# Keeping the high part of u divided by 4096, and writing the low part of the first product's weights at once

## The chip, the cores and the metric

The kernel runs on one core of a Trainium2 chip. The core has TensorE (PE; its weight loads are listed apart as PEld and run beside the products), VectorE (DVE), ScalarE (ACT), GpSimd (POOL) and SyncE (SP), whose queue issues the DMAs. Each engine works through its own queue in order, and engines wait for one another by semaphores. The metric is the device time of one execution in microseconds (us). Five runs of the kernel before gave a median of 676.99 us, from 675.87 to 677.44.

## The reference: what is computed

Two blocks follow each other, all in fp32. The first is attention with a decay, in blocks of 64 positions:

```python
Dmask = np.where(rel >= 0, lam[:, None, None] ** rel[None, :, :], 0.0)
for b in range(nb):
    intra = np.einsum('bhic,bhjc->bhij', qb, kb) * Dmask[None]
    intra = np.einsum('bhij,bhjd->bhid', intra, vb)
    inter = np.einsum('bhid,bhde->bhie', qb * lam_pow[None], kv_state)
    out[:, :, sl] = intra + inter
    kv_state = lam_block * kv_state + np.einsum('bhsd,bhse->bhde', kb_dec, vb)
```

Its result x (4 batches, 768 positions, 512 channels) goes through a low-rank mixer over the positions and a two-layer net over the channels:

```python
h = x.transpose(0, 2, 1) @ U @ V
u = x + h.transpose(0, 2, 1)
ch = np.maximum(u @ w_ch1, 0.0) @ w_ch2
return u + ch
```

The inputs `U`, `V`, `w_ch1` and `w_ch2` are float64 and reach the kernel as pairs of 32-bit words.

## The kernel before, in words

**The split products.** The two large products run in the type fp32r[...]. So each operand is split: for u the high part `t` is u with its low 12 bits cleared (mask `HI`), and the low part is u - t; the weights likewise. With E = 2^-12 the first product u @ w_ch1 is put together from two sums, each in its own PSUM bank:

- `pz` adds w_high * u_high and (4096 w_low) * u_low;
- `pd` adds D_w * D_u, where D_w = w_low - E w_high and D_u = E u_high - u_low.

The result is (1 + E) pz + 4096 pd: multiplied out, the terms that are not wanted cancel, and the four partial products of u and w are left.

**Stages.** There are 24 tiles of 128 positions, s = 0 to 23, six to a batch (NT). Each tile goes through attention (`prep`, `scale`, `scores`, `inter`, `masked`, `intra`, `state`), then through the mixer (`low` once per batch, `low_rows`, `mix`), then through `turn`, which transposes u and splits it. Then the first product runs over 16 blocks of its 2,048 columns (ft) and 6 groups of 512 positions (g), two groups at a time: `hidden(ft, pair)` is one unit of 24 matmuls. Its results (`rs`) go to DRAM and come back for the second product.

**Order.** Up to the end of the first units (`ordered.close()`, L787) the order on each engine is that of the code, written out by hand in `pieces` (L541 to L561): in step s, `prep(s + 1)`, `mix(s - 7)`, `intra(s)`, `state(s)`, `turned`, `scores(s + 1)` and so on. From s = 8 each step also turns one tile. At s = 6, 12 and 18, the first tiles of a batch, the low-rank work of the batch before comes in between: `low` on TensorE, `low_rows` on VectorE (L469), and then `spread` (ScalarE, L480 and L481), `low_part` (VectorE, L475) and `spread_low` (ScalarE, L484). After `ordered.close()` a planner orders the instructions.

**`turn(s)`, L502.** Four transposes write u to PSUM (`pt`), and VectorE masks it into `t`. What follows has two forms. In the first four groups (s = 0 to 15, `g < FG`) VectorE writes the low part from PSUM (L527), and the function `rest` is put off to the next step's `turned`: ScalarE makes `te` = E t (L531) and copies t into the high part `hi` (L532), and GpSimd writes D_u, `diff` = te - low (L533). In the last two groups (s = 16 to 23) VectorE writes D_u (L520), ScalarE copies `hi` (L522) and u itself (L523), and GpSimd makes the low part (L524). `hi` and `low` are slices of the group's tile `u_hl`, 4 runs of 128 elements each, and `diff` of the tile `u_d`; `te` is a tile of its own in the pool slot `tmp`, which has three buffers that `t`, `te`, `uf` and the mixer's `p_h` share.

**The weights.** `weight_steps` (L104) turns the pairs of words into fp32: two masks on VectorE (L153, L154), two ScalarE steps for the exponent (L159, L160), three more on VectorE (L170, L178, L183). `split_steps` (L189) adds the split for w_ch1 and w_ch2 alike: `five` masks the high part (L201) and has ScalarE copy it into the weight tile (L204), `six` subtracts in place (L208) and has ScalarE write 4096 times the result (L209), `seven` makes D_w (L212). The w_ch1 tiles have three buffers (`w1_pool`), the w_ch2 tiles go to DRAM and come back. In attention `aside` issues these steps, and `on_scalar` puts their ScalarE part off to `late` of a following step.

**`hidden`, L695.** After the 16 `pz` matmuls of a unit (L709) ScalarE scales `pz` into `rs` (L715); after the 8 `pd` matmuls (L719) VectorE adds 4096 `pd` (L724), and SP stores the result (L725). The PSUM banks alternate from unit to unit.

Of the kernel before, what the change touches and what calls it, by code (L numbers as in the profile page):

```python
# [8 lines left out]
FP32 = mybir.dt.float32  # L9
# [3 lines left out]
ALU = mybir.AluOpType  # L13

P = 128
# [3 lines left out]
def kernel(  # L19
# [9 lines left out]
    moe_w_ch2: bass.AP,  # L29
    out: bass.AP,  # L30
):

# [12 lines left out]
    nc = tc.nc  # L47
# [16 lines left out]
    E = 2.0**-12  # L64
# [15 lines left out]
    def on_scalar(what):  # L80
        if late and late[0] is None:
            late.append(what)
        else:
            what()
# [12 lines left out]
    def tmp(name):  # L97
        return wconv.tile([P, C], FP32, tag="tmp", bufs=3, name=name)
# [87 lines left out]

        return fetches + [one, two, three, four]

    def split_steps(tile_of, src, in_parts=False):  # L189

        st = {}

        def dst():
            if "w" not in st:
                st["w"] = wconv.tile([P, C], FP32, tag="wf", name="wf")
            return st["w"]

        def five():
            st["t"] = t = wconv.tile([P, C], FP32, tag="wt", name="wt")
            st["o"] = o = tile_of()  # L200
            nc.vector.tensor_scalar(  # L201
                t.bitcast(U32), st["w"].bitcast(U32), HI, None, ALU.bitwise_and
            )
            on_scalar(lambda: nc.scalar.copy(o[:, 0, :], t))  # L204

        def six():
            w = st["w"]
            nc.vector.tensor_tensor(out=w, in0=w, in1=st["t"], op=ALU.subtract)  # L208
            on_scalar(lambda: nc.scalar.mul(st["o"][:, 1, :], w, 4096.0))  # L209

        def seven():
            nc.vector.scalar_tensor_tensor(  # L212
                st["o"][:, 2, :], st["t"], -E, st["w"], ALU.mult, ALU.add
            )

        return weight_steps(dst, src, C, in_parts=in_parts) + [five, six, seven]
# [3 lines left out]
    def w1_steps(ft, in_parts=False):  # L220
        def tile_of():
            w1v[ft] = w1_pool.tile([P, 3, C], F32R, tag="w1", name="w1")
            return w1v[ft]

        cols = moe_w_ch1[:, ft * P : (ft + 1) * P].rearrange("(c p) f -> p c f", p=P)
        return split_steps(tile_of, cols, in_parts)
# [3 lines left out]
    keep = mix_ctx.enter_context(tc.tile_pool(name="keep", bufs=1, side="right"))  # L230
# [12 lines left out]
    def one_bank(shape, name, tag):  # L243
        return psf.tile(shape, FP32, tag=tag, name=name)
# [4 lines left out]
    def bank(shape, name, tag):  # L249
        return psa[0].tile(shape, FP32, tag=tag, bufs=2, name=name)  # L250
# [72 lines left out]
    st = {}  # L323
# [178 lines left out]
    def turn(s):  # L502

        g, n = divmod(s, TG)
        if n == 0:
            uhl[g] = hl_at[g >= FG].tile([P, 2, CT, N], F32R, tag="hl", name="u_hl")
            ud[g] = d_at[g >= FG].tile([P, CT, N], F32R, tag="d", name="u_d")
        cols = slice(n * P, (n + 1) * P)
        pt = one_bank([P, CT, P], "put", "pt") if g < FG else bank([P, CT, P], "put", "b1")
        for ct in range(CT):  # L510
            nc.tensor.transpose(  # L511
                out=pt[:, ct, :], in_=xs[s][:, ct * P : (ct + 1) * P], identity=ident
            )
        nc.sync.dma_start(out=u_d[s], in_=xs.pop(s))
        t = tmp("ut").rearrange("p (c n) -> p c n", n=P)
        nc.vector.tensor_scalar(t.bitcast(U32), pt.bitcast(U32), HI, None, ALU.bitwise_and)
        hi, low, diff = uhl[g][:, 0, :, cols], uhl[g][:, 1, :, cols], ud[g][:, :, cols]
        if g >= FG:

            nc.vector.scalar_tensor_tensor(diff, t, 1.0 + E, pt, ALU.mult, ALU.subtract)  # L520
            uf = tmp("uf").rearrange("p (c n) -> p c n", n=P)
            nc.scalar.copy(hi, t)  # L522
            nc.scalar.copy(uf, pt)  # L523
            nc.gpsimd.tensor_tensor(out=low, in0=uf, in1=t, op=ALU.subtract)  # L524
            return

        nc.vector.tensor_tensor(out=low, in0=pt, in1=t, op=ALU.subtract)  # L527

        def rest():
            te = tmp("te").rearrange("p (c n) -> p c n", n=P)  # L530
            nc.scalar.mul(te, t, E)  # L531
            nc.scalar.copy(hi, t)  # L532
            nc.gpsimd.tensor_tensor(out=diff, in0=te, in1=low.bitcast(FP32), op=ALU.subtract)  # L533

        turned[s] = rest

# [5 lines left out]
    for s in range(NS):  # L542
        b, c = divmod(s, NT)
# [20 lines left out]
    def load_next(name, engine=nc.sync):  # L564
# [5 lines left out]
        "prep": prep, "fade": fade, "scores": scores, "masked": masked, "inter": inter,  # L570
        "intra": intra, "state": state,
        "low": low, "low_rows": low_rows, "next_of_low": next_of_low, "mix": mix, "turn": turn,
        "scale": scale, "turned": lambda s: turned.pop(s)(),
    }
# [112 lines left out]
    def banks(n, other):  # L687

        tags = ("b1", "b2") if other else ("a1", "a2")
        pzs, pds = ([bank([P, N], name, tag) for i in range(n)] for name, tag in zip(("pz", "pd"), tags))  # L690
        return list(zip(pzs, pds))
# [3 lines left out]
    def hidden(ft, pair, before={}):  # L695

        acc = dict(zip(pair, banks(len(pair), next(turns))))
        count = iter(range(12 * len(pair)))

        def others():  # L700
            for what, s in before.get(next(count), ()):
                run[what](s)

        w = w1v[ft].rearrange("p n (c f) -> p n c f", f=P)
        for ct in range(CT):
            for n in range(2):
                for g in pair:
                    others()
                    nc.tensor.matmul(  # L709
                        out=acc[g][0], lhsT=w[:, n, ct, :], rhs=uhl[g][:, n, ct, :],  # L710
                        start=(ct == 0 and n == 0), stop=(ct == CT - 1 and n == 1),
                    )
        rs = {g: r_pool.tile([P, N], FP32, tag="r", name="r") for g in pair}
        for g in pair:
            nc.scalar.mul(rs[g], acc[g][0], 1.0 + E)  # L715
        for ct in range(CT):
            for g in pair:
                others()
                nc.tensor.matmul(  # L719
                    out=acc[g][1], lhsT=w[:, 2, ct, :], rhs=ud[g][:, ct, :],  # L720
                    start=(ct == 0), stop=(ct == CT - 1),
                )
        for g in pair:
            nc.vector.scalar_tensor_tensor(rs[g], acc[g][1], 4096.0, rs[g], ALU.mult, ALU.add)  # L724
            nc.sync.dma_start(out=r_d[ft][g], in_=rs[g])  # L725

    def w2_steps(ft):
        def tile_of():
            w2v[ft] = w2_pool.tile([P, 3, C], F32R, tag="w2", name="w2")
            return w2v[ft]  # L730

        def keep():
            nc.sync.dma_start(out=w2_d[ft], in_=w2v.pop(ft).bitcast(FP32))

        return split_steps(tile_of, moe_w_ch2[ft * P : (ft + 1) * P, :]) + [keep]


    w2hl, w2dd = {}, {}
# [15 lines left out]
    def run_units(units, side, every=lambda i: None):  # L754
        for i, (pair, ft) in enumerate(units):
            hidden(ft, pair)
            for step in side[len(side) * i // len(units) : len(side) * (i + 1) // len(units)]:
                step()
            every(i)
# [18 lines left out]
    for i, (pair, ft) in enumerate(head):  # L778
        before = {}
        for unit, n, *piece in rest:  # L780
            if unit == i:
                before.setdefault(n, []).append(piece)
        hidden(ft, pair, before)
        for n, step in side:
            if n == i:
                step()
# [9 lines left out]
    for ft in range(3, FT - 1):  # L796
        side += w1_steps(ft) + w2_steps(ft - 3)
    side += w2_steps(FT - 4)
    run_units(body, side)
    side = w1_steps(FT - 1)  # L800
    for ft in range(LAST, FT):
        side += w2_steps(ft)
# [8 lines left out]
    rs, ms = {}, {}  # L811
# [17 lines left out]
    acc = {}  # L829
# [50 lines left out]
    for i, (pair, ft) in enumerate(tail[6:]):  # L880
        hidden(ft, pair)
        if i < 2:
            for n in range(2):
                w2_back(backs.pop(0))
        if i == 0:
            for n in range(3):
                fetch(n)
        if i == 1:
            for n in range(2):
                split(n)  # L890

    STAG = 3
    for i in range(len(steps) - STAG):
        g, ft = steps[i]
# [49 lines left out]
```

## Time and profile before

| What | us |
|---|---|
| Median of five runs | 676.99 |
| The profiled execution, its whole time | 676.99 |
| Its span, first to last instruction | 674.9 |
| Attention and mixer, up to the first `pz` matmul | 0 to 123.4 |
| First product, its units alone | 152 to 400.2 |
| Second product | 400.5 to the end |

How to read the profile: times are from the start of the span. A row of a group gives line, engine, operation, output and input by the program's names, shape and count, then the busy time and the mean of one in ns, then the idle time just before them and what ended it. The chain of waits is followed back from the last instruction: at each step to what released it, or to its predecessor on the same engine. A row of the timeline gives start, length, engine, line and what is computed; consecutive instructions of one kind are drawn together (x32), and a bracket names idle time before the row and what ended it. The ends of matmuls are modelled, so starts are the surer numbers.

Two more groups of the page, the longest on VectorE and ScalarE, belong to the second product and to the first one's `rs`:

```profile
L825 DVE SCALAR_TENSOR_TENSOR m<-rm,m 128x512 fp32r<-128x512 f32 x96 | 71.5, 746 | 47.5 <-ACT m L824 47.1
...
L715 ACT ACTIVATE r<-pz 128x512 f32<-128x512 f32 x96 | 52.0, 593 | 58.8 <-PE pz L709 58.2
```

The granted TensorE clock was full throughout (mean 1.000).

### The profile page before, as it was taken

The page shows a single profiled execution, that of the slowest core. Times are in us where ns is not written, and L with a number is a line of the kernel's source. Part 1 is how long each engine was busy: PE and PEld are TensorE (multiplying, and loading weights), DVE is VectorE, ACT ScalarE, POOL GpSimd, SP SyncE. Part 2 cuts the span into 40 slices and gives each one's busy share as a digit, 9 for nine tenths or more (in the row PEclk, how much of TensorE's full clock was granted, in tenths as well). Part 3 has the DMA queues.
Part 4 walks back from the last instruction along what each step waited for, and adds up shares of the span by engine and source line. Part 5 has one row for each costly group of instructions (what it writes and reads, how often), then busy time and mean ns, then how long its engine had stood idle before and what let it go on. Part 6 is the DMA issues. An engine that isn't in the chain of part 4 may idle for free.

```text
span 674.9 us, 13222 instructions
## 1 busy us (share of the span) xinstructions
PE 666.5 (99%) x5124; PEld 545.3 (81%) x5124; DVE 499.5 (74%) x879; ACT 293.1 (43%) x545; POOL 113.8 (17%) x92
## 2 busy tenths in 40 slices
PE   9999999999999999999999999999999999999997
PEld 8988898787888888888888888888888888888885
DVE  4689999777999777777797255786686776865864
ACT  4666878555665544444455121232232322322320
POOL 4556667330000000000000000030030300300300
PEclk9999999999999999999999999999999999999999
DMA  9999884164777655555577999854363363543521
GB/s 206 218 234 240 216 220 126 62 224 155 239 261 242 223 202 203 202 203 203 202 266 255 327 322 388 287 171 148 96 210 102 110 203 94 163 149 95 169 81 63
DMA packets 131776, 131.28 MB, mean 195 GB/s; under 512 B 81346, under 2 KB 89794, under 8 KB 131714
## 3 DMA queue, kind: packets, MB, share of 16 engines
q1 hardware_dynamic: 130656, 130.18, 61.1%
q8 instruction: 40, 0.66, 0.4%
q10 hardware_dynamic: 1058, 0.26, 0.2%
q14 instruction: 22, 0.18, 0.1%
HBM read 80.09 MB, written 50.33 MB: 193 GB/s over the span
## 4 chain that ended last, share of the span: by engine, by line
PE 94%; DVE 3%; ACT 2%; issue 0%; DVEq 0%; ACTq 0%
PE pz L709 27%; PE pz L843 13%; PE pz L841 13%; PE pd L719 13%; PE pd L845 13%; PE pss L388 3%; PE px L441 3%; PE put L511 2%; PE pq L343 1%; PE pkv L406 1%; PE px L429 1%; PE pk L343 1%; PE pp L456 1%; PE pu L494 1%; DVE sm L397 1%
## 5 line engine op out<-in xcount | busy, mean ns | idle before, releaser
L709 PE MATMUL pz<-u_hl,w 128*128 128x512 f32 x768 | 190.5, 397 | 0.0
L709 PEld LDWEIGHTS pz<-u_hl,w 128*128 128x128 f32 x768 | 144.0, 188 | 35.5 <-issue 0.4
L841 PE MATMUL pz<-w_hl,m 128*128 128x512 f32 x384 | 151.6, 396 | 0.0
L843 PE MATMUL pz<-w_hl,m 128*128 128x512 f32 x384 | 151.6, 396 | 0.0
L845 PE MATMUL pd<-w_d,m 128*128 128x512 f32 x384 | 150.0, 396 | 0.0
L824 ACT ACTIVATE m<-mt 128x512 fp32r<-128x512 f32 x96 | 60.7, 632 | 196.8 <-PE pd L845 138.5
L825 DVE SCALAR_TENSOR_TENSOR m<-rm,m 128x512 fp32r<-128x512 f32 x96 | 71.5, 746 | 47.5 <-ACT m L824 47.1
L870 POOL TENSOR_TENSOR o<-o,u 128x512 f32<-128x512 f32 x20 | 29.8, 1524 | 447.4 <-DVE o L866 447.4
L724 DVE SCALAR_TENSOR_TENSOR r<-pd,r 128x512 f32<-128x512 f32 x96 | 61.8, 686 | 53.2 <-ACT r L715 43.6
L719 PE MATMUL pd<-u_d,w 128*128 128x512 f32 x384 | 98.6, 397 | 0.0
L843 PEld LDWEIGHTS pz<-w_hl,m 128*128 128x128 f32 x384 | 72.3, 188 | 17.7
L845 PEld LDWEIGHTS pd<-w_d,m 128*128 128x128 f32 x384 | 72.3, 188 | 17.6
L841 PEld LDWEIGHTS pz<-w_hl,m 128*128 128x128 f32 x384 | 72.3, 188 | 17.6
L719 PEld LDWEIGHTS pd<-u_d,w 128*128 128x128 f32 x384 | 72.1, 188 | 17.3
L715 ACT ACTIVATE r<-pz 128x512 f32<-128x512 f32 x96 | 52.0, 593 | 58.8 <-PE pz L709 58.2
L823 DVE TENSOR_SCALAR mt<-rm 128x512 uint32<-128x512 uint32 x96 | 46.2, 481 | 33.0 <-DMA rm<-r_d 32.7
L826 DVE SCALAR_TENSOR_TENSOR m<-m 128x512 fp32r<-128x512 f32 x96 | 69.1, 720 | 0.9
L204 ACT CAST w<-wt 128x512 fp32r<-128x512 f32 x32 | 19.9, 622 | 40.9 <-DVE wt L201 33.7
L397 DVE TENSOR_TENSOR sm<-pss,mask 128x512 f32<-128x512 f32 x48 | 30.8, 683 | 5.8 <-PE pss L388 5.7
L371 POOL TENSOR_TENSOR qs<-qt,powq 128x512 f32<-128x512 f32 x20 | 26.0, 1298 | 24.3 <-ACT qt L346 21.9
L159 ACT ACTIVATE sc<-sc,ends 128x512 f32<-128x512 uint32 x30 | 21.7, 723 | 18.3 <-DVE sc L153 18.3
L441 PEld LDWEIGHTS px<-vraw,sm 128*64 128x64 f32 x768 | 24.6, 137 | 5.9 <-issue 2.6
(84 smaller groups left out, 710.8 us busy)
## 6 DMA issues: line engine op xcount, KB each, us to landing
r_d<-r SPq DMA_DIRECT2D x96, 256.0 KB, 2.5
rm<-r_d SPq DMA_DIRECT2D x96, 256.0 KB, 2.7
words<-in_moe_w_ch_dram SPq DMA_DIRECT2D x30, 512.0 KB, 4.4
w_d<-w SPq DMA_DIRECT2D x16, 768.0 KB, 3.3
w_hl<-w_d SPq DMA_DIRECT2D x16, 512.0 KB, 6.2
vraw<-in_v_dram SPq DMA_DIRECT2D x24, 256.0 KB, 4.3
u_d<-x_nat SPq DMA_DIRECT2D x24, 256.0 KB, 3.4
u<-u_d SPq DMA_DIRECT2D x24, 256.0 KB, 3.9
```

Of the source, the lines that this page charges most:

```text
L441: nc.tensor.matmul(out=px[half[t], x, a, :], lhsT=sm[:, x, a, half[t]], rhs=vr[:, 2 * a + x, :], start=(first and a == 0), stop=(a == HP - 1),
L709: nc.tensor.matmul(out=acc[g][0], lhsT=w[:, n, ct, :], rhs=uhl[g][:, n, ct, :], start=(ct == 0 and n == 0), stop=(ct == CT - 1 and n == 1),)
L715: nc.scalar.mul(rs[g], acc[g][0], 1.0 + E)
L719: nc.tensor.matmul(out=acc[g][1], lhsT=w[:, 2, ct, :], rhs=ud[g][:, ct, :], start=(ct == 0), stop=(ct == CT - 1),)
L724: nc.vector.scalar_tensor_tensor(rs[g], acc[g][1], 4096.0, rs[g], ALU.mult, ALU.add)
L823: nc.vector.tensor_scalar(t.bitcast(U32), r.bitcast(U32), HI, None, ALU.bitwise_and)
L824: nc.scalar.activation(out=m[:, 0], in_=t, func=AF.Relu)
L825: nc.vector.scalar_tensor_tensor(m[:, 1], r, 0.0, hi, ALU.max, ALU.subtract)
L826: nc.vector.scalar_tensor_tensor(m[:, 2], hi, E, low, ALU.mult, ALU.subtract)
L841: nc.tensor.matmul(out=pz, lhsT=m[:, 0, cols], rhs=hl[:, 0], start=first, stop=False)
L843: nc.tensor.matmul(out=pz, lhsT=m[:, 1, cols], rhs=hl[:, 1], start=False, stop=end)
L845: nc.tensor.matmul(out=pd, lhsT=m[:, 2, cols], rhs=dd, start=first, stop=end)
```

## The change

The high part of u is kept as E u_high, made by one ScalarE multiplication in place of the copy, in both forms of `turn`. GpSimd then takes the high part itself to make D_u, and `te` is gone. In turn the low part of w_ch1 is kept as it is, not times 4096, so both terms of `pz` are smaller by 4096, and `rs` is scaled by 4096 + 1 instead of 1 + E. Since it needs no factor any more, VectorE's subtraction in `six` writes the low part of w_ch1 straight into the weight tile, and `seven` reads it from there. For w_ch2 nothing changes: `w2_steps` passes scale=4096.0 and keeps the ScalarE step.

```diff
-    def split_steps(tile_of, src, in_parts=False):
+    def split_steps(tile_of, src, in_parts=False, scale=None):
...
         def six():
-            w = st["w"]
-            nc.vector.tensor_tensor(out=w, in0=w, in1=st["t"], op=ALU.subtract)
-            on_scalar(lambda: nc.scalar.mul(st["o"][:, 1, :], w, 4096.0))
+            w, low = st["w"], st["o"][:, 1, :]
+            st["low"] = low.bitcast(FP32) if scale is None else w
+            nc.vector.tensor_tensor(
+                out=low if scale is None else w, in0=w, in1=st["t"], op=ALU.subtract
+            )
+            if scale is not None:
+                on_scalar(lambda: nc.scalar.mul(low, w, scale))

         def seven():
             nc.vector.scalar_tensor_tensor(
-                st["o"][:, 2, :], st["t"], -E, st["w"], ALU.mult, ALU.add
+                st["o"][:, 2, :], st["t"], -E, st["low"], ALU.mult, ALU.add
             )
...
-            nc.scalar.copy(hi, t)
+            nc.scalar.mul(hi, t, E)
             nc.scalar.copy(uf, pt)
...
         def rest():
-            te = tmp("te").rearrange("p (c n) -> p c n", n=P)
-            nc.scalar.mul(te, t, E)
-            nc.scalar.copy(hi, t)
-            nc.gpsimd.tensor_tensor(out=diff, in0=te, in1=low.bitcast(FP32), op=ALU.subtract)
+            nc.scalar.mul(hi, t, E)
+            nc.gpsimd.tensor_tensor(
+                out=diff, in0=hi.bitcast(FP32), in1=low.bitcast(FP32), op=ALU.subtract
+            )
...
-            nc.scalar.mul(rs[g], acc[g][0], 1.0 + E)
+            nc.scalar.mul(rs[g], acc[g][0], 4096.0 + 1.0)
...
-        return split_steps(tile_of, moe_w_ch2[ft * P : (ft + 1) * P, :]) + [keep]
+        rows = moe_w_ch2[ft * P : (ft + 1) * P, :]
+        return split_steps(tile_of, rows, scale=4096.0) + [keep]
```

## The prediction

> **What bounds the kernel now.** I read the busy shares first, then the shares of the chain that ended last.
>
> ```profile
> PE 666.5 (99%) x5124; PEld 545.3 (81%) x5124; DVE 499.5 (74%) x879; ACT 293.1 (43%) x545; POOL 113.8 (17%) x92
> ...
> PE 94%; DVE 3%; ACT 2%; issue 0%; DVEq 0%; ACTq 0%
> ```
>
> TensorE is the bound: it is busy nearly throughout, and the chain runs over it for 94% of the span. So time can only come from the other 6%. The chain in order of time shows where that lies: from 105.08 to the last VectorE additions at 669.93 every piece is a TensorE piece (a pair of two products, 24 matmuls, takes 3.75 + 1.88 = 5.62 us, over and over). ScalarE stands in the chain between 41 and 105 us only. The place to see is the start of the third batch of attention (s = 12). The next lines are the chain there: start, length, what.
>
> ```profile
> 70.34 0.62 ACT vp L481
> 70.99 0.63 ACT te L531
> 71.62 0.51 ACT u_hl L532
> 72.13 0.02 issue
> 72.15 0.61 ACT vp L484
> ...
> 73.05 0.81 ACT faded L380 x3
> 73.85 0.47 ACT qt L346
> 74.32 0.49 ACT kt L346
> ```
>
> ScalarE runs without a gap, `te` among its work, and TensorE's `pkv` waits for the last piece: `pkv` takes the PSUM bank that the `kt` copy empties. The timeline of TensorE beside it (a bracket is idle time and its releaser):
>
> ```profile
> 72.02 0.60 PE L343 MATMUL pk<-ident,kraw 128*128 128x128 f32 x4
> 72.82 0.50 PE L494 MATMUL pu<-vp 128*128 128x512 f32 x1 [0.20 <-ACT vp L484]
> 73.25 1.15 PE L441 MATMUL px<-vraw,sm 128*64 128x64 f32 x32
> 74.86 0.69 PE L406 MATMUL pkv<-vraw,ks 128*64 128x64 f32 x16 [0.46 <-ACT kt L346]
> ```
>
> In an undisturbed step (s = 15, `pk` at 82.64, `px` at 83.40) `pu` starts 0.36 us after `pk` and `pkv` 0.98 us after `px`. Here it is 0.80 and 1.61, so 0.44 and 0.63 us are lost to ScalarE.
>
> **Removing `te` (16 ScalarE multiplications, s = 0 to 15).** Their group and the nearest rows for what replaces them:
>
> ```profile
> L531 ACT ACTIVATE te<-ut 128x512 f32<-128x512 f32 x16 | 10.2, 635 | 0.0
> L532 ACT CAST u_hl<-ut 128x512 fp32r<-128x512 f32 x16 | 9.7, 609 | 0.0
> L209 ACT ACTIVATE w<-wf 128x512 fp32r<-128x512 f32 x32 | 20.2, 633 | 0.0
> L533 POOL TENSOR_TENSOR u_d<-te,u_hl 128x512 fp32r<-128x512 f32 x16 | 24.3, 1520 | 12.7 <-ACT te L531 11.0 <-DVE kv L414 1.7
> L524 POOL TENSOR_TENSOR u_hl<-uf,ut 128x512 fp32r<-128x512 f32 x8 | 10.3, 1290 | 17.3 <-ACT uf L523 17.3
> ```
>
> `te` takes 0.635 us but overlaps its successor: at 70.99 the next starts 0.54 later. The scaled high part takes `te`'s place in the queue and is of L209's form (0.633), so GpSimd's wait ends when it does now, and what comes after on ScalarE moves up by 0.54 (0.53 where no wait lies between). The same 0.53 is free in the other thirteen steps, where ScalarE waits for TensorE anyway: worth nothing. Three places count:
>
> - **s = 9 to 10.** `kt` ends at 58.00 + 0.58 = 58.58 and `pkv` starts at 58.63. `px` began at 57.43, so TensorE could start `pkv` at 57.43 + 0.98 = 58.41. `kt` would end at 58.05: gain 58.63 - 58.41 = 0.22. TensorE is late next.
> - **s = 12 to 13.** L484 would start at 71.61, after its input (the four L475 end at 71.41), and end at 72.22; `pu` starts at its own 72.02 + 0.36 = 72.38. But `px` does not gain with it: `sm` (L397) ends at 71.90 + 1.29 = 73.19, and at s = 9, where `px` was held by `sm`, its last 28 matmuls began 0.06 after `sm` ended and `pkv` came 0.87 later. That allows `pkv` at 74.12. `kt` would end at 74.23 - 0.54 + 0.58 = 74.27, `pkv` start at 74.32: gain 0.54.
> - **s = 18 to 19.** The same form. `kt` would end at 104.45 - 0.54 + 0.58 = 104.49; `sm` ends at 102.38 + 1.29 = 103.67, so `px` allows 103.67 + 0.06 + 0.87 = 104.60. `pkv` moves from 105.08 to 104.60: gain 0.48, and VectorE's `sm` is late next.
>
> Sum: 0.22 + 0.54 + 0.48 = 1.24 us. Nothing takes it back by this trace: in the steps after each place the chain is TensorE alone, and `sm` keeps 0.11 us of room at the tightest (ends 78.50, `px` 78.67).
>
> **A rule against this sum.** The Trainium skill, Perfetto Trace Analysis, Identifying the Most-Contended Engine, says to find the engine with the highest occupancy and optimize that first. ScalarE at 43% is far from it, and the change takes no matmul away: by the rule alone the gain is 0. The rows above say 1.24, since ScalarE ends the wait at three places that the average hides. I follow the rows.
>
> **GpSimd reads the high part instead of `te`.** `te` lay in one piece; the high part lies in four runs of 128, as the low part and D do. No row has both inputs cut. Nearest: L524, both inputs in one piece, 1.29; L533 with one cut, 1.28 where VectorE leaves it alone (1.73 at worst). The first cut cost nothing, so I take 0 for the second. Bounds: 0 below (the output was cut already) and 0.45 above (1.73 - 1.28). Who would pay: at s = 8 VectorE's L154 takes 1.49 instead of 0.42 us, ending just after this GpSimd instruction (49.60 to 51.06), and TensorE's `px` waits for the `sm` behind it; there each added 0.1 us costs 0.1. Elsewhere a step holds 1.29 + 1.06 + 1.73 = 4.08 us of GpSimd in 4.74.
>
> **s = 16 to 23.** The copy becomes a multiplication, 0.621 to 0.633: 8 x 0.012 = 0.1 us on a ScalarE with gaps of 0.5 to 2 us. Nothing. The changed scalar in `rs` costs nothing either.
>
> **Low part of the first product's weights.** 16 of the 32 L209 go: 16 x 0.53 us of ScalarE. Two lie in attention (81.39 and 116.34), in steps where ScalarE has 0.35 us or more before `qt` or TensorE sets the pace; the rest in the body, where TensorE never waits. Worth 0. VectorE keeps its 32 subtractions; writing fp32r costs nothing by L212 (fp32r, 0.683 median) against L208 (fp32, 0.684). What is added is a wait: the subtraction now writes the weight tile and needs TensorE to have left the slot. ScalarE's L204 waits for that 7 times, 1.0 us at most, so VectorE may too. Queued behind are the weight steps and L724, which itself waits for the end of the same unit. L724 frees a bank that TensorE needs a unit (5.62 us) later. If VectorE lost 1 us seven times the bank would still be in time: 0. SP's queue gets no new instruction. The order in the body isn't the order of the code (L153 of the next tile stands between L201 and L208), so the planner may set it anew; the same 5.62 us covers that.
>
> **Result.** The profiled execution took 676.99 (span 674.9 and 2.1 around it), which is also the median of the runs, so 676.99 - 1.24 = 675.75.
>
> **Rivals.**
> - *No gain* (0.18): 676.9. VectorE is 92 to 93% busy from 60 to 120 us; what ScalarE gives up, VectorE's `kv` and `sm` may keep. Against it: the arithmetic above sets `sm` against `kt` at each place.
> - *More* (0.08): if `px` follows `pu` rather than `sm`, the whole stall at s = 12 goes (1.07) and about as much at s = 18: 0.22 + 1.07 + 1.0 = 2.3, 674.7. Against it: `sm` ends 0.06 before `px`.
> - *Slower: GpSimd's subtraction stretches* (0.16), because both inputs are cut. Place: s = 8, and every step with all three GpSimd instructions. It starts to decide at 4.74 - 4.08 = 0.66 us more per subtraction, when GpSimd becomes the pace of attention. At 1.0 more: 1.0 at s = 8 and 8 steps x 0.34 = 2.7, less 1.24, is 2.5: 679.5. For it: nothing shows two cut inputs. Against: the first cut cost nothing.
> - That the change doesn't do what it says is small: the scaling by 4096 is moved, no product is dropped.
>
> **From cases to numbers.** The forecast has 0.58. Its own spread is 0.8 to 1.8 us of gain; 0.2% is 1.35 us, about what a measurement of this kernel can tell from no change (five runs spread over 1.6). That cuts the forecast into 0.27 faster and 0.31 same. With *more*, faster is 0.35; with *no gain*, same is 0.49; slower 0.16. The range reaches from *more* (674.7) past *no gain* to the bound of 0.45 at s = 8 with a run's scatter on top: 677.7. The forecast's own range is 675.2 to 676.2.
>
> **What would show it.** Right: one ScalarE instruction between `vp` L481 and L484 at the third and fourth batch, `pkv` there 0.5 us sooner after `px`, GpSimd's 16 subtractions still at 1.28 to 1.75, and everything from the first product on moved as a block by about 1.2 us. Wrong: a subtraction above 2 us, an `sm` that ends later against `px` than now, or any TensorE gap after 122 us.

## The result

The changed kernel takes 675.14 us (median of 26 runs, 674.4 to 677.04), the kernel before on the same chip 677.04 (47 runs). The ratio is 0.9973 with a 95% interval of 0.9967 to 0.9979: 1.83 us or 0.27% faster. 1.24 us were forecast.

The changed kernel was profiled three times. The second trace fell in a slow execution, 808.74 us at a granted clock of 0.754, and is left out of every comparison below. The first trace belongs to an execution of 677.72 us, the slowest of all its runs, in which the copies of `x_nat` wait twice for the transfer of u to DRAM, 2.9 us at the longest. What follows is read from the third trace: its first `px` of s = 1 starts at 13.99 us as it does before, so the two can be laid side by side; its granted clock is 1.000, as before. The busy times and the shares of the chain, in the order of the lines shown of before:

```profile
span 673.1 us, 13173 instructions
...
PE 665.9 (99%) x5124; PEld 545.2 (81%) x5124; DVE 498.0 (74%) x879; ACT 277.2 (41%) x513; POOL 113.8 (17%) x92
...
PE 95%; DVE 3%; ACT 1%; DMA 1%; issue 0%; SPq 0%; DVEq 0%; ACTq 0%
```

ScalarE has lost 32 instructions (545 to 513) and 16 us of busy time, TensorE still makes 5124 matmuls, and TensorE holds 95% of the chain instead of 94, ScalarE 1% instead of 2. The 1% of DMA is one transfer of u to DRAM, 45.29 to 48.88 us; it cost nothing, since TensorE's starts around it are those of before to 0.01 us (s = 8 to 10). The chain of waits at the start of the third batch, s = 12 to 13:

```profile
70.08 0.62 ACT vp L486
70.70 0.01 issue
70.71 0.63 ACT u_hl L535
71.34 0.02 issue
71.37 0.60 ACT vp L489
...
73.07 0.47 ACT qt L351
73.54 0.49 ACT kt L351
74.03 0.04 issue
74.07 0.69 PE pkv L411 x16
```

One ScalarE instruction stands between the two `vp`, where there were two. `kt` still ends the wait of `pkv`. TensorE's timeline at the same place:

```profile
72.11 0.47 PE L499 MATMUL pu<-vp 128*128 128x512 f32 x1
72.51 1.50 PE L446 MATMUL px<-vraw,sm 128*64 128x64 f32 x32
74.07 0.69 PE L411 MATMUL pkv<-vraw,ks 128*64 128x64 f32 x16
```

The wait of `pu` for `vp` is gone. `px` begins 0.74 us earlier than before (73.25), but it now takes 1.50 us instead of 1.15: it begins before `sm` is ready and is held in the middle. VectorE's `sm`, first before, then after:

```profile
71.90 1.29 DVE L397 TENSOR_TENSOR sm<-pss,mask 128x512 f32<-128x512 f32 x2
71.63 1.29 DVE L402 TENSOR_TENSOR sm<-pss,mask 128x512 f32<-128x512 f32 x2
```

Before, `sm` ends at 73.19, 0.06 us ahead of `px`. After, it ends at 72.92, 0.41 us behind the start of `px`. At s = 19 it is `sm` that ends last: `kt` is ready at 103.72, and `px` is held until 102.93:

```profile
102.93 1.03 PE L446 MATMUL px<-vraw,sm 128*64 128x64 f32 x28 [0.26 <-DVE sm L402]
103.80 0.66 PE L411 MATMUL pkv<-vraw,ks 128*64 128x64 f32 x16
```

The groups of the edited instructions (busy, mean of one in ns, idle before):

```profile
L536 POOL TENSOR_TENSOR u_d<-u_hl 128x512 fp32r<-128x512 f32 x16 | 24.3, 1521 | 12.9 <-ACT u_hl L535 11.2 <-DVE kv L419 1.7
...
L210 DVE TENSOR_TENSOR w<-wf,wt 128x512 fp32r<-128x512 f32 x16 | 12.1, 758 | 0.0
...
L535 ACT ACTIVATE u_hl<-ut 128x512 fp32r<-128x512 f32 x16 | 10.1, 634 | 0.0
```

GpSimd's subtraction with both inputs cut takes 1521 ns, as it took 1520 with one. VectorE's subtraction into the weight tile has no idle time before it: it never waited for the slot of the weight tile.

How much was gained where is seen from the starts of the matmuls. This table is made from the timelines of TensorE; an offset is the start of `px` (or of the first `pz`) against before, and "wait" is the time from the start of `px` to that of `pkv`, 0.98 where nothing is late:

| | Before: wait | After: wait | After: offset of the next step |
|---|---|---|---|
| s = 9 | 1.46 | 1.46 | 0.01 |
| s = 10 | 1.20 | 0.98 | -0.26 |
| s = 13 | 1.61 | 1.56 | -0.79 |
| s = 19 | 1.61 | 1.46 | -1.30 |
| first `pz` | | | -1.30 |

Three steps down, 0.27, 0.53 and 0.51 us, and nothing between. From the first `pz` to VectorE's last row (two additions of 128 x 256) both take 547.34 us. But the span is 1.87 us shorter, 673.08 against 674.95 (the page prints tenths). The rest lies behind the start of that last row, at 670.73 before and at 669.43 after: 4.22 us to the end against 3.65.

### The profile page after: what moved, and what is told of

It is laid out like the page before. It is cut to its first block, busy times and chain, and to the rows that moved or that the text cites. A ratio compares the mean times of both kernels' runs of the same rounds, so it can differ in the third digit from the quotient of the medians.

```text
span 675.7 us, 13173 instructions
## 1 busy us (share of the span) xinstructions
PE 666.5 (99%) x5124; PEld 545.4 (81%) x5124; DVE 498.9 (74%) x879; ACT 277.4 (41%) x513; POOL 113.4 (17%) x92
## 4 chain that ended last, share of the span: by engine, by line
PE 94%; DVE 3%; ACT 1%; issue 1%; SPq 0%; DMA 0%; POOL 0%; DVEq 0%; POOLq 0%; ACTq 0%
PE pz L714 27%; PE pd L724 13%; PE pz L849 13%; PE pz L847 13%; PE pd L851 13%; PE px L446 3%; PE pss L393 3%; PE put L516 2%; PE pq L348 1%; PE pkv L411 1%; PE px L434 1%; PE pk L348 1%; DVE sm L402 1%; PE pu L499 1%; SPq L140 0%
## 5 line engine op out<-in xcount | busy, mean ns | idle before, releaser
L446 PE MATMUL px<-vraw,sm 128*64 128x64 f32 x768 | 28.2, 225 | 0.7 <-DVE sm L402 0.5
```

What stands on the lines that cost most here:

```text
L446: nc.tensor.matmul(out=px[half[t], x, a, :], lhsT=sm[:, x, a, half[t]], rhs=vr[:, 2 * a + x, :], start=(first and a == 0), stop=(a == HP - 1),
```

## Experiments

The theory on trial was that of the prediction: the gain comes from `te` going at three places, and nothing else of the change counts. The rivals: that the weights or something spread over many steps share in it, or that no single place does. Of single traces the starts have to be taken with care: from run to run the DMA waits of the first tiles shift everything behind by -0.7 to +1.5 us (before itself, profiled again, has lost 1.08 at s = 4, where `px` waits for `vraw`). So offsets are compared from step to step within a trace, and times by the ratios.

**The changed kernel again, and its halves.** `after_again` is the changed kernel as it is. `u_alone` puts ScalarE's instruction back for the low part of w_ch1 (factor 1); `w_alone` puts `te` back, and with it the copy in the second form of `turn` and the factor 1 + E of `rs`:

```diff
 u_alone
...
-            nc.vector.tensor_tensor(
-                out=low if scale is None else w, in0=w, in1=st["t"], op=ALU.subtract
-            )
-            if scale is not None:
-                on_scalar(lambda: nc.scalar.mul(low, w, scale))
+            st["low"] = w
+            nc.vector.tensor_tensor(out=w, in0=w, in1=st["t"], op=ALU.subtract)
+            on_scalar(lambda: nc.scalar.mul(low, w, 1.0 if scale is None else scale))
 w_alone
...
-            nc.scalar.mul(hi, t, E)
-            nc.gpsimd.tensor_tensor(
-                out=diff, in0=hi.bitcast(FP32), in1=low.bitcast(FP32), op=ALU.subtract
-            )
+            te = tmp("te").rearrange("p (c n) -> p c n", n=P)
+            nc.scalar.mul(te, t, E)
+            nc.scalar.copy(hi, t)
+            nc.gpsimd.tensor_tensor(out=diff, in0=te, in1=low.bitcast(FP32), op=ALU.subtract)
...
```

> The changed kernel once more, for a second trace. Theory (ScalarE's te at three places): against the kernel before about 0.9975, and in an execution without DMA waits the first pz matmul starts at about 122.2 us instead of 123.4: pkv at s = 10, 13 and 19 follows px sooner by 0.2, 0.5 and 0.5 us. The first trace of the changed kernel has two waits of x_nat for a u_d store (2.9 and 2.6 us) and starts pz at 124.7; if these waits belong to the change, they return here; if they are the scatter of one execution, they don't.

> The half with u alone: te gone, high part scaled, but the low part of w_ch1 again subtracted in place and copied by ScalarE with factor 1. Theory (te on ScalarE): the whole gain, about 0.9975 of the kernel before and within 0.1% of the changed one. Rival (the weights half brings the gain): 1.000.

> The half with the weights alone: low part of w_ch1 written at once by VectorE; te and the copy of the high part as before. The low part of w_ch1 then lacks its factor 4096 with nothing to balance it, so the numbers differ from the reference. Theory (te on ScalarE): 1.000, within 0.1%. Rival (the weights half): 0.9975.

Measured: the changed kernel again 0.9981 [0.9970, 0.9992]; `u_alone` 0.9978 [0.9968, 0.9989], and in its trace the offset goes from -0.69 to -1.97, a gain of 1.28; `w_alone` 1.0006 [1.0000, 1.0013], its offset staying at +1.33 from s = 7 to the first `pz`. The whole gain is in the half of u; the weights bring nothing.

**The three places alone.** A spare `te` that nothing reads is put behind the high part, in one kernel everywhere but in the three that count, in the other only there. Tile n is turned in step n + 7 and its `rest` comes in step n + 8, so these are tiles 1, 4 and 10, issued in steps 9, 12 and 18, ahead of the `pkv` of s = 10, 13 and 19. Each kernel has one of the two `if` lines:

```diff
+            if s not in (1, 4, 10):        # gone_at_three
+            if s in (1, 4, 10):            # kept_at_three
+                te = tmp("te").rearrange("p (c n) -> p c n", n=P)
+                nc.scalar.mul(te, t, E)
```

> The changed kernel with an unread te multiplication put back behind the high part for 13 of the 16 tiles, all but those issued in steps s = 9, 12 and 18. Theory (three places): still 0.9975, as the changed kernel. Rival (the gain comes from less ScalarE work over all of attention): about 1.000 (0.2 x 13/16 of the gain lost or more).

> The changed kernel with the unread te multiplication put back behind the high part only at the three places (tiles 1, 4 and 10, issued in steps s = 9, 12 and 18); the other 13 stay gone. Theory (three places): the whole gain is lost, 1.000, and px to pkv takes 1.2, 1.6 and 1.6 us again at s = 10, 13 and 19. Rival (less ScalarE work everywhere, or a part of the gain outside these places): 0.9983 or less.

> The kernel before against itself. Every theory: 1.000, and px to pkv takes 1.2, 1.6 and 1.6 us at s = 10, 13 and 19. What it tells: how far a ratio of the same kernel strays, and how far the start of the first tile and the DMA waits of attention move from one execution to the next (first pz matmul at 123.4 us in the first trace).

`gone_at_three`: 0.9978 [0.9969, 0.9986], from +0.12 to -1.16, a gain of 1.28: as much as with all sixteen gone. `kept_at_three`: 0.9994 [0.9984, 1.0004], offset +1.38 to +1.41 from s = 1 to the first `pz`, with `pkv` 1.20, 1.61 and 1.61 us behind `px` again: no gain, though thirteen multiplications are gone. Before against itself: 0.9992 [0.9983, 1.0002], which shows how far a ratio strays. ScalarE's rows in `kept_at_three`, where one spare multiplication stands in the way again:

```profile
72.37 0.63 ACT L535 ACTIVATE u_hl<-ut 128x512 fp32r<-128x512 f32 x1
72.91 0.61 ACT L541 ACTIVATE te<-ut 128x512 f32<-128x512 f32 x1
73.55 0.61 ACT L489 CAST vp<-vp 32x512 fp32r<-32x512 f32 x1
```

And TensorE's there: `pkv` is 1.61 behind `px`, as before.

```profile
74.65 1.15 PE L446 MATMUL px<-vraw,sm 128*64 128x64 f32 x32
76.26 0.69 PE L411 MATMUL pkv<-vraw,ks 128*64 128x64 f32 x16 [0.46 <-ACT kt L351]
```

So the theory's places are shown from both sides.

**What is late next.** At s = 8 `sm` stands behind two weight masks that VectorE does while GpSimd works. `aside_after_8` issues the weight step behind `masked` there instead of ahead of it; `aside_after_three` does so at s = 8, 12 and 18; `aside_and_high` moves the high part (`turned`) behind the last `vp` at the start of a batch as well:

```diff
 aside_after_three
-        step += [("aside", s)] * (done >= 0)
+        step += [("aside", s)] * (done >= 0 and s not in (8, 12, 18))
...
-        step += [("aside", s)] * (done < 0)
+        step += [("aside", s)] * (done < 0 or s in (8, 12, 18))
 aside_and_high, in addition
-        step += [("turned", done - 1)] * (done > 0) + [("late", s)] * (done >= 0)
+        step += [("turned", done - 1)] * (done > 0 and c > 0) + [("late", s)] * (done >= 0)
         step += [("next_of_low", b - 1)] * (c == 0 and b > 0)
+        step += [("turned", done - 1)] * (done > 0 and c == 0)
```

> The changed kernel with the weight steps of s = 8 issued behind sm instead of ahead of it. In the traces so far VectorE's two masks there take 1.03 and 1.49 us instead of 0.42, ending just after GpSimd's ks and u_d, and px of s = 9 waits for the sm behind them (px to pkv 1.46 us). Theory (the masks are held by GpSimd's instructions): px of s = 9 starts 0.2 us sooner and pkv follows after 0.98: 0.7 us less than the changed kernel, about 0.997 of the kernel before. Rival (sm is late for another reason): no change against the changed kernel.

> The same at s = 8, 12 and 18, and at s = 12 and 18 the high part on ScalarE goes behind vp L489. The prediction named sm as next in line there once te is gone, with kt close by: with both moved, px to pkv should fall from 1.57 and 1.46 us to about 1.0 at s = 13 and 19. Theory: 1.6 us less than the changed kernel, about 0.9955 of the kernel before. Rival (ScalarE or another engine is next in line): not below aside_after_8.

`aside_after_8`: 0.9968 [0.9959, 0.9977], in its trace the offset goes from -0.61 to -2.61: 2.0 us, 0.7 more than the change. VectorE's timeline at s = 8, after the change and with the masks moved:

```profile
48.91 1.03 DVE L154 TENSOR_SCALAR sc<-words 128x512 uint32<-128x512 uint32 x1
49.85 1.49 DVE L155 TENSOR_SCALAR m<-words 128x512 uint32<-128x512 uint32 x1
51.27 1.27 DVE L402 TENSOR_TENSOR sm<-pss,mask 128x512 f32<-128x512 f32 x2
```

```profile
48.97 1.29 DVE L402 TENSOR_TENSOR sm<-pss,mask 128x512 f32<-128x512 f32 x2 [0.60 <-PE pss L393]
50.17 0.42 DVE L154 TENSOR_SCALAR sc<-words 128x512 uint32<-128x512 uint32 x1
50.51 0.42 DVE L155 TENSOR_SCALAR m<-words 128x512 uint32<-128x512 uint32 x1
```

GpSimd beside them, first after the change, then with the masks moved:

```profile
48.59 1.06 POOL L365 TENSOR_TENSOR ks<-kraw,small 128x512 f32<-128x512 f32 x1 [0.32 <-POOL qs L376]
49.61 1.46 POOL L536 TENSOR_TENSOR u_d<-u_hl 128x512 fp32r<-128x512 f32 x1
```

```profile
48.99 1.27 POOL L536 TENSOR_TENSOR u_d<-u_hl 128x512 fp32r<-128x512 f32 x1
```

The masks go from 0.42 to 1.03 and 1.49 us when they start beside GpSimd's instructions, and each ends 0.27 to 0.29 us after the one beside it (`ks` at 49.65, `u_d` at 51.07). `sm`, which reads PSUM, takes 1.27 to 1.29 for two in either place, also beside `u_d`, and GpSimd's subtraction then takes 1.27. That agrees with the Trainium skill (SBUF — State Buffer, Who interferes with whom): VectorE and GpSimd share a port pair, whichever comes first has it for its whole instruction, and a VectorE instruction with at most one SBUF input outside its two-port modes never contends. In which mode the masks ran, no run here shows.

The edit takes away the masks' place in the queue and their stretching together. By these rows it is the stretching that counts: at the spacing that the moved masks have (0.34 us), two masks from 48.91 on would let `sm` start at 49.59 and end near 50.9, an estimate, ahead of the `px` of s = 9. TensorE there, after the change and with the masks moved:

```profile
52.00 0.34 PE L446 MATMUL px<-vraw,sm 128*64 128x64 f32 x4
52.60 1.03 PE L446 MATMUL px<-vraw,sm 128*64 128x64 f32 x28 [0.26 <-DVE sm L402]
```

```profile
51.16 1.15 PE L446 MATMUL px<-vraw,sm 128*64 128x64 f32 x32
```

Moved, `px` follows 0.4 us behind `pu` instead of 0.6 and runs through.

`aside_and_high` was a miss: 0.9969 [0.9958, 0.9980], its offset from +0.09 to -1.27, a gain of 1.36 where about 2.9 were forecast, and less than with the masks at s = 8 alone. ScalarE's timeline there:

```profile
69.47 0.62 ACT L486 CAST vp<-p_h 32x512 fp32r<-32x512 f32 x1
70.56 0.62 ACT L489 CAST vp<-vp 32x512 fp32r<-32x512 f32 x1 [0.48 <-DVE vp L480]
71.20 0.63 ACT L535 ACTIVATE u_hl<-ut 128x512 fp32r<-128x512 f32 x1
```

In its old place the high part fills the wait of 0.48 us for VectorE's `vp`. Moved, it leaves that empty and pushes `kt` back: `pkv` comes 1.89 us behind `px` at s = 13 and 19 (1.56 and 1.46 after the change). The forecast had taken the high part for something that could be moved at no cost.

> The changed kernel a third time. Theory (three places): 0.998 of the kernel before, and in a trace without DMA waits of x_nat px to pkv takes 0.98, 1.57 and 1.46 us at s = 10, 13 and 19, while px of s = 13 starts about 0.5 us and px of s = 19 about 0.3 us sooner against the steps ahead of them than in the kernel before: 1.28 us in all by the first pz matmul, as in the half with u alone.

> The changed kernel with the weight steps of s = 8, 12 and 18 behind sm, the high part left where the change puts it. Theory (at s = 13 kt holds pkv by about 0.2 us over sm; at s = 19 sm is last): sm moves up by 0.4 to 0.7 us there, so px starts and ends sooner, but pkv still waits for kt: nothing at s = 13, at most 0.1 us at s = 19; so level with the one that moves s = 8 alone. Rival (sm is what is last at both): 0.4 us and more at each, 0.9958.

> The same, and GpSimd makes faded for s = 13 and 19 in one instruction, where ScalarE took four (0.97 us) between vp L489 and qt. If kt is last at both places, it comes 0.97 us sooner, sm and kt both leave the way, and px to pkv falls to 1.0 us: 0.5 us each, about 1.0 us less than the kernel with s = 8, 12 and 18 moved. If GpSimd's queue is late (u_d ahead of faded, qs behind it), kv or qs takes its place and nothing is gained.

The last of these takes one of ScalarE's works away, at s = 7, 13 and 19 alone:

```diff
+            if s % NT == 1 and s > NT:
+                nc.gpsimd.tensor_tensor(
+                    out=faded, in0=kv[s], in1=lamc.broadcast_to([P, HP, D]), op=ALU.mult
+                )
+                return
             for a in range(HP):
                 nc.scalar.mul(faded[:, a, :], kv[s][:, a, :], lamc[:, a, :])
```

On one chip: the changed kernel 0.9971 [0.9963, 0.9980], `aside_after_three` 0.9970 [0.9960, 0.9979], and `faded_on_gpsimd` 0.9966 [0.9957, 0.9975], 674.37 us, the lowest median here. In its trace `aside_after_three` gains 1.94 us, 0.70 of it at s = 9; the weight steps moved at s = 12 and 18 brought nothing, since `kt` is late there (0.53 and 0.44 us at s = 13 and 19, against 0.53 and 0.51).

`faded_on_gpsimd` gains 2.59 us in its trace, and its `pkv` stands 0.98 behind `px` at s = 13 and 19, and at s = 7 too (1.43 before and after the change). But of the 1.0 us forecast for s = 13 and 19 only 0.15 came; 0.49 came at s = 7, which the forecast left out. At s = 14 and 20 TensorE waits anew, 0.23 and 0.50 us. The rows at s = 14, of TensorE, VectorE and GpSimd:

```profile
74.76 0.69 PE L439 MATMUL px<-kv,qs 64*64 64x64 f32 x32 [0.23 <-DVE kv L424]
...
73.61 0.68 DVE L507 TENSOR_TENSOR x_nat<-pu,x_nat 128x512 f32<-128x512 f32 x1
74.20 0.41 DVE L424 TENSOR_TENSOR kv<-pkv,faded 128x256 f32<-128x256 f32 x1
...
72.04 0.80 POOL L385 TENSOR_TENSOR faded<-kv,powq 128x256 f32<-128x256 f32 x1
```

GpSimd's product is ready at 72.84. `kv` starts at 74.20, behind the earlier work in VectorE's queue, which has no gap from 70.54 on. So VectorE, not GpSimd, is late next. The intervals of these kernels overlap; that the two beat the change is seen in the traces, not in the times.

**The half microsecond at the end.** In the three traces with 13207 or more instructions (before, before again, `w_alone`) VectorE's last row starts 4.22, 3.90 and 4.20 us ahead of the end; in the nine others, with 13172 to 13188, 3.64 to 3.67. The view of the DMA queues over 2 us, from just before the last output transfers move, first before (672.0 to 674.0; the row of GB/s has 40 slices of 0.05 us):

```profile
GB/s 143 246 287 532 348 287 348 205 144 123 185 307 328 389 348 328 328 205 82 41 21 20 21 20 20 41 20 20 20 0 0 0 0 0 0 0 0 0 0 0
...
q14 instruction: 1, 0.01, 1.0%
```

Then the changed kernel, 670.7 to 672.7:

```profile
GB/s 143 266 307 410 348 307 348 246 164 103 164 307 369 348 369 348 348 185 144 21 0 0 0 0 0 0 0 0 0 0 0 0 0 0 0 0 0 0 0 0
```

Before, a piece of the program itself (q14, instruction) is fetched among these transfers, and their last packets drip in at 20 GB/s for 0.45 us more; afterwards no piece is fetched. At 20 GB/s a slice of 0.05 us holds some 1,000 bytes, about one packet (288 packets carry 0.26 MB), so one packet at a time is still under way. The piece itself takes 1.0% of 16 engines over 2 us, 0.32 us of one engine. Both would fit a single DMA engine that fell behind. The same single piece is there in the two other long ends. SP's wait for the transfers, in the view of SP's waits, is 1.8 us before (the longest 1.6) and 1.3 after (0.8). The last kernel brings the number of instructions back with 49 spare ones in ScalarE's idle time:

```diff
         for g in pair:
             nc.scalar.mul(rs[g], acc[g][0], 4096.0 + 1.0)
+            if ft >= 6 and left:
+                left.pop()
+                nc.scalar.mul(spares[0], rs[g][:, 0:2], 1.0)
...
```

> The changed kernel with 49 spare ScalarE instructions (128 x 2, read by nothing), one behind each of the first 49 scalings of r from group ft = 6 on, where ScalarE has long idle stretches; 13173 + 49 = 13222 instructions, as many as before. *Fetch theory*: the half microsecond that the first twelve traces leave over lies behind the last VectorE instruction, where the kernels with 13207 and more instructions still fetch one or two pieces of program (q14, 22 pieces in all) beside the last output transfers, and those with 13188 and fewer (q14, 21 pieces) fetch none. Then this kernel has 22 pieces or more, at least one of them in the last 5 us, its last two output transfers land in 2.1 to 2.4 us instead of 1.8, and from the start of the last VectorE instruction to the end of the span it takes 3.9 to 4.3 us instead of 3.65; the gain up to the first pz stays (pkv behind px as in the changed kernel), and the ratio rises from 0.9971 by 0.0004 to 0.0009, to about 0.9978. *Rival*: the end has to do with the removed instructions themselves, not with the length of the program; then 3.6 to 3.7 us and a ratio of about 0.9971. Between the two if the pieces come at another place: 22 pieces, but none in the last 5 us, and 3.65 us.

The in-between case came: 22 pieces are fetched as before, but the additional one earlier, at 655.2 us, some 20 us before the end, and the end is short, 3.67 us. The ratio is 0.9964 [0.9951, 0.9977]. So neither more instructions nor one more piece lengthens the program by itself. What goes with the half microsecond, in 3 traces of 13 and in no other, is a piece fetched just then, 2.8 us before the end each time. `kept_at_three` agrees: it gains nothing at the three places and has the short end, which alone would be 0.57 of 677 us or 0.9992; it measured 0.9994, though its interval reaches past 1. That the piece causes the drip fits the time and place, but no run moved a piece into the end on purpose: it stays an inference.

## Why the prediction was right

- **The three places.** Forecast 0.22 + 0.54 + 0.48 = 1.24; the trace has 0.27 + 0.53 + 0.51 = 1.30, and the two kernels that part these places from the other thirteen give 1.28 and 0. What is late next was named right: TensorE itself at s = 10, `kt` still at s = 13, `sm` at s = 19, with `kt` ready 0.08 us ahead of `pkv`.
- **`px` does not gain with it** was right in its result and loose in its words: `px` does begin sooner, by 0.48 more than at s = 12, and is then held in its middle by `sm`. For `pkv` that comes to the same. So two of the signs were worded wrongly: the wait from `px` to `pkv` shrank by 0.05 and 0.15 us and not by 0.5, because `px` moved along, and "an `sm` that ends later against `px`" was to mean wrong, yet it came with the forecast gain.
- **The same 0.53 in thirteen other steps is worth nothing.** Right: `kept_at_three` has them all, and gains 0.0.
- **GpSimd's second cut input.** Taken at 0 between bounds of 0 and 0.45; measured 1274 to 1735 ns over 16, against the 1279 to 1746 of before, with a median of 1538 in both. The slower rival, a stretched subtraction, never came near its 0.66 us.
- **Weights.** Right at 0: `w_alone` 1.0006. The added wait for the weight slot did not occur at all, and the write in fp32r has the same median, 682 ns against 684. The planner did set the body anew, and it cost nothing: 547.34 us from the first `pz` on in both.
- **Rule against row.** By the rule of the most contended engine, as the prediction read it, the gain would be 0; the rows said 1.24. Work of ScalarE, at 43% of the span, was worth 1.3 us, because it ended TensorE's wait in three steps. What was gained is idle time of the busiest engine itself, so the two disagree only if shares are read without the waits.
- **What was missing** is a term: the end of the program. The prediction took all behind the last matmul as unchanged, and 0.57 us went there: 1.30 + 0.57 = 1.87, which is the difference of the two spans and close to the 1.83 of the ratio. The piece of program among the last transfers stood in the trace of before.
- **Range and chances.** The forecast's own range was 675.2 to 676.2, a gain of 0.8 to 1.8. The measured 675.14 and 1.83 lie just beyond it, inside the wider range that the case *more* had opened at 674.7. The end, which nobody had reckoned with, fell into room made for something else: that the total stayed within the wider range is in part luck, while the three places were right in mechanism and size. The largest single chance (0.49) was put on a difference within 0.2%. By the matmuls alone, 1.3 us or 0.19%, it would have fallen there; with the end it is 0.27%, and the interval of this measurement lies beyond the bound (0.21 to 0.33%).

## What to carry to other kernels

An engine with a low average can still set the pace in a few steps; walk the chain of waits to where its pieces stand back to back, and move each later instruction by what is taken out, until another input becomes the latest. Then count only those places: thirteen of sixteen removed instructions brought nothing here. And before moving an instruction, look whether it fills a wait: the high part cost nothing where it stood, and 0.3 us a step where it didn't.

## What was not expected of the hardware

- Two VectorE masks of 128 x 512, reading and writing SBUF, took 0.42 us each by themselves and 1.03 and 1.49 beside GpSimd's instructions, each ending 0.3 us after the one beside it. `sm`, with one input in PSUM, was not slowed. Putting the masks behind `sm` was worth 0.7 us, over half of what `te` had cost.
- Inputs in four runs of 128 instead of one piece cost GpSimd's subtraction nothing: the median of 16 is 1538 ns with one input cut and with both.
- A piece of program fetched during the last output transfers goes with an end that is 0.2 to 0.6 us longer; one fetched some 20 us ahead of the end does not.
- The waits for DMAs in the first tiles, and in one execution for u's transfer to DRAM, move single executions by over 1 us, as much as the change is worth. The first pair of traces, 676.99 and 677.72 us, shows the wrong sign.
